# All steps of a recurrent attention and gated feed-forward kernel in another order

## The chip, the cores and the metric

The kernel runs on one core of a Trainium2 chip, from inputs in device memory to outputs in device memory, as one program. The metric is the device time of one execution in microseconds. Three runs of the kernel before took 202.21, 202.94 and 203.57 us; the median is 202.94.

## The reference

A linear attention with a per-channel decay (RWKV-6 form) is followed by a gated feed-forward layer. For 4 batches, 8 heads, 768 time steps and a head width of 48, the attention is

```python
for t in range(S):
    cur = np.einsum('bhd,bhe->bhde', u[None] * kt, vt)
    y[:, :, t] = np.einsum('bhd,bhde->bhe', rt, state + cur)
    state = wt[:, :, :, None] * state + np.einsum('bhd,bhe->bhde', kt, vt)
```

Its output, heads joined to rows of 384 (3072 rows), goes through

```python
rms = np.sqrt(np.mean(x * x, axis=-1, keepdims=True) + 1e-06)
xn = x / rms * rms_g
g = xn @ w_gate                       # 384 x 1536
silu = g * (1.0 / (1.0 + np.exp(-g)))
val = xn @ w_val                      # 384 x 1536
return (silu * val @ w_out)           # 1536 x 384
```

## The kernel before

**Tiles.** Time is cut into six superblocks of 128 steps (n = 0 to 5). A superblock holds the four batches (j = 0 to 3), so 4 x 128 = 512 rows go through the feed-forward layer together. The state of each batch is carried from one superblock to the next.

**Steps of the attention, per n and j.** `load_w`, `load_k`, `load_r`, `load_v` fetch 128 steps (lines 244 and 257; the first four `load_w` fetch superblocks 0 and 1 at once, all on SP's queue). `ln` takes the logarithm of w on ScalarE; `cs_mm` sums it along time on TensorE (for n of 2 and up `cs_add` on VectorE makes the second sum); `exp_r` and `exp_k` (ScalarE) turn the sums into factors, and `r_mul` and `k_mul` apply them (VectorE; `k_mul` on GpSimd for n of 1 and up). The products are transposed: for n = 0 and 1 by TensorE and a copy of ScalarE (`rk_pe`, `rk_tr`), later by a transposing DMA on SP's queue (`rk_tr`, line 474). `q_mm` multiplies them within the block, `q_mask_e`, `q_copy_o` and `q_mask_o` mask the result into SBUF; `cast_v` makes a bf16 copy of v (on ScalarE for n = 0 and 1, else on GpSimd); `y_mm` multiplies the masked result by it and adds the old state's part; `st_mm` and `st_new` make the new state. The term with u goes over `bonus_mul` (GpSimd, two products), `bonus_sum` (VectorE) and `bonus_v` (GpSimd), and `x_add` adds it to y.

**Norm.** `x_sq` (ScalarE), `x_rstd` (GpSimd, ScalarE for n = 0) and `xn_mul` (ScalarE) scale the rows; `xn_pe` with `xn_out` (n up to 3), or the transposing DMA `xn_tr` (line 563) with `xn_gain` on GpSimd (n = 4 and 5), put them transposed into `xnt`. A feed-forward step of superblock n needs the `xnt` of all four batches.

**Feed-forward, per n and f = 0 to 11** (columns of the weights in 12 parts of 128). `gate_mm` and `val_mm` are three matmuls of 128x512 each (line 598), called a group here; `silu` (ScalarE) and `h_mul` (VectorE) make `ht`. `o_mm` (line 630) multiplies all 12 parts of `ht` of one batch by `w_out` in 12 matmuls; `o_out` and `out_dma` copy and store it. The weights come by GpSimd's queue: `load_gv.g.h` (line 346) fetches a small piece (g = 0, f = 0 to 3) or a large one (g = 1, f = 4 to 11) of the gate (h = 0) or value (h = 1) weights, `load_wo` (line 352) the output weights.

**Zero matmuls.** `warm` (line 369) multiplies a tile of zeros and its result is not used. There are 48.

**What sets the order.** The string `ORDER` (lines 25 to 129) lists the 1106 steps one behind the other, and the loop of line 649 records them so. Nothing reorders them afterwards: each engine, SP's DMA queue included, takes its own steps in the order of the list and waits at each for what that step needs. Two other things follow from the list. The buffers of the pools are handed out in turn (eight for each of the loads of r, k and v, four for w). And `psum` (line 218) picks for each result of TensorE a bank that, by the list, has had its last use: two banks serve `cs_mm` and `gate_mm` (ring a), two `cs_mm`, `cs_add` and `val_mm` (b), four all else (q). So a `gate_mm` waits until the `silu` of the gate two before has emptied its bank.

`act` (line 227) puts an ACT_TABLE_LOAD ahead of a function of ScalarE that isn't in the table loaded last; `ln` and the exponentials are in one, `silu` in the other:

```python
def act(table_name, **kw):
    if table[0] != table_name:
        nc.scalar.preload_act_table_set(table_name)
        table[0] = table_name
```

## Time and profile before

| | |
|---|---|
| three runs, us | 202.21, 202.94, 203.57 |
| profiled execution: span from the first to the last instruction, us | 202.2 |
| TensorE busy, share of the span | 95% |
| VectorE, ScalarE, GpSimd busy | 72%, 68%, 66% |
| mean granted TensorE clock | 0.999 |
| read from device memory, written | 25.96 MB, 4.72 MB |
| function table loads of ScalarE | 10 |
| zero matmuls | 48 |

The profiled execution's span (202.2 us) is as long as the shortest run's time, so nothing that lies around the span has to be added to it. A row of a timeline or of the chain begins with the start and the duration in microseconds from the start of the span, then engine, line, operation, the tile written and the tiles read, and how many instructions stand in the row; in brackets is the idle time of the engine before it and what ended it. Matmuls are pipelined: their durations overlap, so their cost is read from one start to the next, or from the chain, which counts only the time that each adds. The rows of groups give the count, the busy time and the mean duration in nanoseconds, then the idle time in front and what ended most of it. "SPq" is SP's queue of DMA issues; a DMA issued by GpSimd is a row of GpSimd.

### The profile page before, as it was taken

The numbers are of one execution on the slowest core, as the hardware profiler recorded it, in microseconds if no ns is written. First come the engines' busy times: TensorE is split into PE (matmuls) and PEld (weight loads), VectorE is DVE, ScalarE is ACT, GpSimd is POOL, SyncE is SP. The second block draws the span as 40 slices with busy tenths as digits, with TensorE's granted clock in tenths as the row PEclk, the third lists the DMA queues.
The fourth block names the chain that finished last, engine by engine and source line by source line (L and its number), as shares of the span: only waits on it lengthen the run. The fifth ranks groups of instructions, "written<-read, shape, count | busy, mean of one in ns | idle before, by whom it ended". The sixth has DMA issues, their size and how long they took to land.

```text
span 202.2 us, 4444 instructions
## 1 busy us (share of the span) xinstructions
PE 192.6 (95%) x1600; PEld 113.5 (56%) x1600; DVE 146.1 (72%) x289; ACT 136.6 (68%) x278; POOL 134.3 (66%) x198
## 2 busy tenths in 40 slices
PE   1999988899999999999999999999999999999994
PEld 1564655455666555665556665555555555555562
DVE  6257796658999699987988889788878972146521
ACT  2577699688998557997566978679867764046300
POOL 6527599658789966899789898859898742400000
PEclk9999999999999999999999999999999999999999
DMA  6999999989999999958999978996184022103022
GB/s 152 243 244 177 209 182 202 202 161 201 199 192 221 196 179 238 225 133 194 177 231 245 206 171 195 216 241 134 24 192 112 15 68 71 45 3 117 0 97 99
DMA packets 121566, 32.41 MB, mean 160 GB/s; under 512 B 116420, under 2 KB 120392, under 8 KB 121544
## 3 DMA queue, kind: packets, MB, share of 16 engines
q1 hardware_dynamic: 119504, 28.58, 67.2%
q0 software_dynamic: 2032, 3.54, 9.7%
q8 instruction: 12, 0.20, 0.4%
q14 instruction: 10, 0.08, 0.1%
q10 hardware_dynamic: 8, 0.00, 0.0%
HBM read 25.96 MB, written 4.72 MB: 152 GB/s over the span
## 4 chain that ended last, share of the span: by engine, by line
PE 79%; SPq 8%; DMA 8%; POOL 2%; issue 1%; ACT 0%; POOLq 0%
PE ps_av L598 12%; PE ps_bu L598 12%; PE ps_bv L598 10%; PE ps_au L598 10%; PE ps_qx L630 8%; PE ps_qv L630 7%; SPq L244 7%; DMA wg_sb<-in_moe_w_gate_dram 6%; PE ps_qz L630 5%; PE ps_qu L630 3%; SPq L257 2%; DMA kt<-in_k_dram 2%; PE ps_qu L487 1%; PE ps_av L406 1%; PE ps_qu L515 1%
## 5 line engine op out<-in xcount | busy, mean ns | idle before, releaser
L630 PEld LDWEIGHTS <-ht 128*128 128x128 bf16 x300 | 28.3, 98 | 16.9
L231 ACT ACTIVATE sg<-ps_av 128x512 bf16<-128x512 f32 x38 | 22.7, 598 | 18.4 <-PE ps_av L598 16.8
L616 DVE TENSOR_TENSOR ht<-ps_bu,sg 128x512 bf16<-128x512 f32 x38 | 26.1, 686 | 11.7 <-PE ps_bu L598 8.4
L598 PEld LDWEIGHTS <-wg_sb 128*128 128x128 bf16 x216 | 22.8, 114 | 20.2 <-DMA wg_sb<-in_moe_w_gate_dram 2.1
L598 PEld LDWEIGHTS <-wv_sb 128*128 128x128 bf16 x216 | 23.2, 114 | 19.3 <-DVE xnt L580 0.2
L616 DVE TENSOR_TENSOR ht<-ps_bv,sg 128x512 bf16<-128x512 f32 x34 | 23.3, 686 | 12.2 <-PE ps_bv L598 8.8
L452 POOL TENSOR_TENSOR ruk<-rt,kt 128x384 f32<-128x384 f32 x24 | 24.0, 1000 | 11.1 <-DMA kt<-in_k_dram 6.0
L598 PE MATMUL ps_av<-xnt,wg_sb 128*128 128x512 bf16 x114 | 30.9, 380 | 0.4 <-DMA wg_sb<-in_moe_w_gate_dram 0.4
L231 ACT ACTIVATE sg<-ps_au 128x512 bf16<-128x512 f32 x34 | 20.4, 599 | 16.0 <-PE ps_au L598 14.6
L598 PE MATMUL ps_bu<-xnt,wv_sb 128*128 128x512 bf16 x114 | 30.9, 380 | 0.0
L598 PE MATMUL ps_au<-xnt,wg_sb 128*128 128x512 bf16 x102 | 27.7, 381 | 0.8 <-DMA wg_sb<-in_moe_w_gate_dram 0.8
L598 PE MATMUL ps_bv<-xnt,wv_sb 128*128 128x512 bf16 x102 | 27.7, 380 | 0.0
L453 POOL TENSOR_TENSOR ruk<-ruk,u_bc 128x384 f32<-128x384 f32 x24 | 23.9, 997 | 1.9
L462 POOL TENSOR_TENSOR ydiag<-vt,diag 128x384 f32<-128x384 f32 x24 | 19.7, 830 | 0.9 <-DVE diag L457 0.8
L446 POOL TENSOR_TENSOR rk<-kt,ek 128x384 bf16<-128x384 f32 x20 | 19.9, 1003 | 0.3 <-ACT ek L231 0.3
L505 POOL TENSOR_SCALAR_AFFINE_SELECT qts<-qts 128x512 bf16<-128x512 bf16 x20 | 12.5, 636 | 10.7 <-ACT qts L498 10.7
L630 PE MATMUL ps_qx<-wo_sb,ht 128*128 128x384 bf16 x96 | 16.9, 326 | 0.0
L630 PE MATMUL ps_qv<-wo_sb,ht 128*128 128x384 bf16 (+1 forms) x96 | 15.9, 316 | 0.0
L558 ACT ACTIVATE xn<-xb,rstd 128x384 bf16<-128x384 f32 x24 | 14.1, 608 | 1.2 <-POOL rstd L554 1.2
L457 DVE TENSOR_REDUCE diag<-ruk 128x8 f32<-128x384 f32 x24 | 12.9, 543 | 2.7 <-POOL ruk L453 2.7
L231 ACT ACTIVATE lw<-wt 128x384 bf16<-128x384 f32 (+1 forms) x20 | 11.2, 579 | 4.6 <-DMA wt<-in_w_dram 4.5
L229 ACT ACT_TABLE_LOAD x10 | 12.8, 1283 | 1.8 <-PEq L667 1.6
(153 smaller groups left out, 368.2 us busy)
## 6 DMA issues: line engine op xcount, KB each, us to landing
rt<-in_r_dram SPq DMA_DIRECT2D x24, 192.0 KB, 3.9
kt<-in_k_dram SPq DMA_DIRECT2D x24, 192.0 KB, 3.9
vt<-in_v_dram SPq DMA_DIRECT2D x24, 192.0 KB, 3.7
out_dram<-ob SPq DMA_DIRECT2D x23, 192.0 KB, 2.1
wt<-in_w_dram SPq DMA_DIRECT2D x16, 192.0 KB, 3.9
wt<-in_w_dram SPq DMA_DIRECT2D x4, 384.0 KB, 4.6
wo_sb<-in_moe_w_out_dram POOLq DMA_DIRECT2D x3, 384.0 KB, 5.2
wg_sb<-in_moe_w_gate_dram POOLq DMA_DIRECT2D x1, 768.0 KB, 12.0
```

Of the source, the lines that this page charges most:

```text
L229: nc.scalar.preload_act_table_set(table_name)
L231: return nc.scalar.activation(**kw).ins
L244: dmas["load_" + which, n, j] = nc.sync.dma_start(out=inp[which, n, j], in_=t[j, :, n * L:(n + 1) * L, :].rearrange("h t d -> t h d")).ins
L446: eng.tensor_tensor(out=rk[:, n % 2, j, 1, :, 0:D], in0=inp["k", n, j], in1=bank["cs_k", n, j][:, 0:DM].rearrange("p (h d) -> p h d", h=H) ...
L452: nc.gpsimd.tensor_tensor(out=ruk[n, j], in0=inp["r", n, j], in1=inp["k", n, j], op=ALU.mult)
L453: nc.gpsimd.tensor_tensor(out=ruk[n, j], in0=ruk[n, j], in1=u_bc, op=ALU.mult)
L457: nc.vector.tensor_reduce(out=diag[n, j].rearrange("p h o -> p (h o)"), in_=ruk[n, j], axis=mybir.AxisListType.X, op=ALU.add)
L462: nc.gpsimd.tensor_tensor(out=ydiag[n, j], in0=inp["v", n, j], in1=diag[n, j].to_broadcast([128, H, D]), op=ALU.mult)
L558: nc.scalar.activation(out=xn, in_=xb[n, j], func=AF.Copy, scale=rstd[n, j][:, 1:2])
L598: nc.tensor.matmul(ps, lhsT=units(ws, c, f), rhs=xnt[n][:, c, :], start=(c == 0), stop=(c == KC - 1))
L616: nc.vector.tensor_tensor(out=ht[n][:, f, :], in0=bank.pop(("v", n, f)), in1=bank.pop(("sg", n, f)), op=ALU.mult)
L630: nc.tensor.matmul(ps[:, cols], lhsT=ht[n][:, f, b * L:(b + 1) * L], rhs=wo_sb[:, f, cols], start=(f == 0), stop=(f == FC - 1))
```

## The change

The list is replaced by another of 1092 steps. All steps that compute, load or store are in both; the new one has 34 `warm` for 48. Everything else in the kernel is the same text, but the banks and buffers follow the new list.

- The 16 loads of superblock 0 come ahead of all loads of superblock 1 (before, two loads of superblock 1, `load_r.1.3` and `load_k.1.0`, stood ahead of the last, `load_k.0.3`). Batches of superblock 0 are taken in sequence 0, 1, 2, 3 (before 1, 0, 2, 3). The loads of v of superblock 1 are numbers 19, 26, 27 and 28 of SP's queue.
- GpSimd issues the weights as gate small, value small, gate large, value large (before: value small, gate small, gate large, value large); `bonus_v` of batches 2 and 3 of superblock 0 stands ahead of the first.
- The first feed-forward step is `gate_mm.0.1`, before it was `val_mm.0.2`. More attention steps of superblock 1 stand among the first groups.
- `ln.3.0`, `ln.3.1`, `ln.4.1` and `ln.5.1` stand among the `silu` of the superblock before: 16 table loads for 10.
- Of the four `o_mm.4`, two stand behind the first part of superblock 5's feed-forward steps.

The diff replaces all 105 lines of the list; here are the places spoken of:

```diff
-load_r.0.1 load_w.0.1 load_k.0.0 load_k.0.1 ln.0.1 warm.31.0 load_w.0.0 ln.0.0 warm.0.0 warm.13.0 warm.28.0
-bonus_mul.0.1 bonus_sum.0.1 load_r.0.0 load_v.0.0 bonus_mul.0.0 load_w.0.2 load_w.0.3 warm.29.0 load_k.0.2 load_v.0.1
-load_r.0.2 bonus_mul.0.2 load_r.0.3 load_v.0.3 load_v.0.2 bonus_v.0.1 load_r.1.3 load_k.1.0 cs_mm.0.1 exp_k.0.1
...
-rk_pe.0.1 warm.15.0 warm.14.0 load_k.0.3 bonus_mul.0.3 load_r.1.1 load_r.1.0 load_k.1.1 load_v.1.1 load_r.1.2 ln.0.3
-load_k.1.3 warm.20.0 warm.37.0 warm.2.0 warm.22.0 warm.23.0 warm.5.0 warm.3.0 rk_pe.0.0 warm.24.0 load_gv.0.1
-load_k.1.2 load_v.1.0 load_w.2.1 warm.25.0 load_v.1.2 load_w.2.0 load_v.1.3 load_r.2.1 load_r.2.0 load_w.2.2 warm.32.0
...
-exp_r.1.2 w_tot.1.2 r_mul.1.2 w_tot.1.3 bonus_mul.1.3 val_mm.0.2 val_mm.0.3 warm.46.0 gate_mm.0.2 gate_mm.0.3 rk_tr.1.1
-q_mm.1.1 silu.0.2 h_mul.0.2 load_k.2.0 silu.0.3 h_mul.0.3 bonus_sum.1.3 st_new.1.1 gate_mm.0.0 val_mm.0.1 rk_tr.1.0
-bonus_mul.1.0 val_mm.0.0 load_r.2.3 silu.0.0 q_mask_e.1.1 h_mul.0.0 bonus_mul.1.1 bonus_sum.1.1 gate_mm.0.6 silu.0.6
...
-gate_mm.4.10 silu.4.10 val_mm.4.10 h_mul.4.10 val_mm.4.11 h_mul.4.11 o_mm.4.1 o_mm.4.0 o_mm.4.2 x_rstd.5.2 xn_mul.5.2
-x_rstd.5.3 xn_mul.5.3 xn_tr.5.3 xn_tr.5.2 xn_gain.5.2 xn_gain.5.3 out_dma.3.3 xn_gain.5.1 o_mm.4.3 gate_mm.5.5 silu.5.5
...
+warm.0.0 warm.1.0 load_w.0.0 load_k.0.0 ln.0.0 load_w.0.1 cs_mm.0.0 warm.2.0 warm.3.0 warm.4.0 load_r.0.0 load_r.0.1
+exp_r.0.0 ln.0.1 cs_mm.0.1 load_w.0.2 r_mul.0.0 exp_k.0.0 w_tot.0.0 k_mul.0.0 load_k.0.1 rk_pe.0.0 warm.5.0 warm.6.0
...
+bonus_v.0.2 load_r.1.2 load_v.1.0 x_rstd.0.0 bonus_sum.0.3 cast_v.0.3 bonus_v.0.3 w_tot.1.1 st_new.0.0 q_mm.0.3
...
+xn_mul.0.1 load_k.1.0 load_r.1.1 y_mm.0.3 warm.32.0 x_sq.0.2 x_add.0.3 load_gv.0.0 x_sq.0.3 load_r.1.3 load_gv.0.1
+k_mul.1.1 xn_pe.0.1 cs_mm.1.2 x_rstd.0.2 r_mul.1.1 st_new.0.2 x_rstd.0.3 xn_mul.0.2 exp_r.1.2 xn_out.0.1 xn_pe.0.0
+xn_mul.0.3 k_mul.1.0 exp_k.1.2 st_mm.1.0 cs_mm.1.3 xn_pe.0.2 exp_r.1.3 xn_out.0.0 st_mm.0.3 warm.33.0 load_gv.1.0
+w_tot.1.2 xn_out.0.2 load_k.1.2 xn_pe.0.3 rk_pe.1.1 r_mul.1.2 xn_out.0.3 load_v.1.1 load_gv.1.1 load_v.1.3
...
+rk_pe.1.0 gate_mm.0.1 gate_mm.0.3 st_new.1.0 q_mm.1.1 silu.0.1 rk_pe.1.3 gate_mm.0.0 load_w.2.3 silu.0.3 val_mm.0.1
+load_r.2.0 bonus_mul.1.2 gate_mm.0.2 q_mask_e.1.1 rk_tr.1.3 val_mm.0.3 bonus_sum.1.0 rk_tr.1.0 q_copy_o.1.1 silu.0.2
+load_k.2.1 q_mm.1.0 h_mul.0.1 bonus_mul.1.1 val_mm.0.0 h_mul.0.3 q_mm.1.3 q_copy_o.1.0 load_w.2.2 rk_pe.1.2
+bonus_sum.1.1 val_mm.0.2 silu.0.0 q_mask_o.1.1 load_r.2.1 cast_v.1.1 q_mask_e.1.0 bonus_mul.1.3 y_mm.1.1 h_mul.0.0
+q_copy_o.1.3 load_r.2.2 gate_mm.0.5 rk_tr.1.2 h_mul.0.2 st_mm.1.1 bonus_v.1.1 gate_mm.0.6 q_mask_e.1.3 x_add.1.1
...
+gate_mm.1.5 val_mm.1.5 load_k.3.1 st_mm.2.0 silu.1.5 q_mask_o.2.0 val_mm.1.3 h_mul.1.5 gate_mm.1.11 st_new.2.0
+rk_tr.2.3 val_mm.1.8 bonus_v.2.3 h_mul.1.3 silu.1.8 ln.3.0 ln.3.1 gate_mm.1.4 y_mm.2.1 h_mul.1.8 silu.1.11 y_mm.2.0
+x_add.2.1 cast_v.2.2 val_mm.1.4 bonus_sum.2.2 st_mm.2.2 val_mm.1.11 bonus_v.2.0 load_r.3.0 silu.1.4 cast_v.2.3
+gate_mm.1.9 x_sq.2.1 x_add.2.0 st_new.2.2 out_dma.0.1 x_sq.2.0 load_r.3.1 x_rstd.2.1 load_k.3.3 load_r.3.2 silu.1.9
...
+val_mm.2.6 bonus_v.3.3 bonus_v.3.0 y_mm.3.0 val_mm.2.8 rk_tr.3.2 h_mul.2.6 load_k.4.3 val_mm.2.5 st_mm.3.2 ln.4.1
...
+gate_mm.4.7 y_mm.5.2 xn_tr.5.0 x_sq.5.3 x_rstd.5.1 silu.4.8 h_mul.4.0 val_mm.4.7 x_rstd.5.3 x_add.5.2 silu.4.7
+xn_mul.5.1 h_mul.4.7 x_sq.5.2 x_rstd.5.2 gate_mm.4.9 val_mm.4.8 xn_tr.5.1 gate_mm.4.10 val_mm.4.10 xn_mul.5.3
+xn_gain.5.0 h_mul.4.8 val_mm.4.9 silu.4.10 h_mul.4.10 xn_gain.5.1 xn_mul.5.2 xn_tr.5.3 silu.4.9 xn_tr.5.2 xn_gain.5.3
+h_mul.4.9 xn_gain.5.2 o_mm.4.1 o_mm.4.2 gate_mm.5.1 gate_mm.5.6 val_mm.5.6 silu.5.6 val_mm.5.1 gate_mm.5.2 silu.5.1
...
```

174 lines of the change are left out of this document (82 added, 92 removed).

## The prediction

> **What bounds the kernel now.** I read the page first, for the span, the busy shares and the chain that ended last.
>
> ```profile
> span 202.2 us, 4444 instructions
> ...
> PE 192.6 (95%) x1600; PEld 113.5 (56%) x1600; DVE 146.1 (72%) x289; ACT 136.6 (68%) x278; POOL 134.3 (66%) x198
> ...
> PE 79%; SPq 8%; DMA 8%; POOL 2%; issue 1%; ACT 0%; POOLq 0%
> ```
>
> TensorE is busy 95% of the span and makes up 79% of the chain; what is not TensorE there is loading and its issue. The chain in order of time says where each of them stands. From 39.90 to 199.3 us it holds nothing but matmuls, one behind the other. Two of its pieces give the pace:
>
> ```profile
> 163.58 0.65 PE ps_bu L598 x3
> ...
> 168.12 1.95 PE ps_qz L630 x12
> ```
>
> A group of three gate or value matmuls costs 0.65 us, twelve output matmuls of one batch cost 1.95 us. In that stretch there is no gap for an order to close; it can only open new ones. All that can be won lies ahead of it, and TensorE's timeline shows how little stands there:
>
> ```profile
> 33.19 0.81 PE L598 MATMUL ps_bu<-xnt,wv_sb 128*128 128x512 bf16 x3
> ...
> 34.48 0.33 PE L369 MATMUL ps_qz<-zero 128*128 128x384 bf16 x1
> 35.64 0.84 PE L598 MATMUL ps_au<-xnt,wg_sb 128*128 128x512 bf16 x3 [0.83 <-DMA wg_sb<-in_moe_w_gate_dram]
> ...
> 39.90 0.84 PE L598 MATMUL ps_av<-xnt,wg_sb 128*128 128x512 bf16 x3 [0.38 <-DMA wg_sb<-in_moe_w_gate_dram]
> ```
>
> The first value group runs at 33.19, the first gate group waits for its weights until 35.64, the first gate group of the second piece of weights until 39.90. Between 33.19 and 39.90 (6.71 us) the list holds seven groups (7 x 0.65) and one q_mm (0.33, next rows): 4.9 us. So 1.8 us are waiting. The smaller prices that I need, from the timeline:
>
> ```profile
> 37.06 0.23 PE L487 MATMUL ps_qz<-rkT 48*128 48x128 bf16 x1
> ...
> 37.39 0.84 PE L598 MATMUL ps_au<-xnt,wg_sb 128*128 128x512 bf16 x3
> ```
>
> and from the chain:
>
> ```profile
> 43.13 0.45 PE ps_qz L469 x8
> ...
> 156.85 0.17 PE ps_qv L532 x4
> 157.02 0.20 PE ps_qv L535 x8
> ```
>
> A q_mm of one batch takes 0.33 us (37.06 to 37.39), an rk_pe 0.45, a y_mm of a later superblock 0.17 + 0.20 = 0.37.
>
> **Zero matmuls.** Fourteen fewer. Two neighbours:
>
> ```profile
> 12.82 0.33 PE L369 MATMUL ps_qx<-zero 128*128 128x384 bf16 x1
> 12.98 0.33 PE L369 MATMUL ps_qz<-zero 128*128 128x384 bf16 x1
> ```
>
> They start 0.16 us apart, so 2.2 us of TensorE go. All stand ahead of 34.5 us, where TensorE waits for data anyway: I count nothing.
>
> **Loads and the weights' issue.** TensorE's work ahead of the first group is the same set in both orders: all of superblock 0, the running sums of superblock 1, two rk_pe and one st_mm of it. What can move is when that group starts. The weights are issued by GpSimd, in line with its products:
>
> ```profile
> 22.47 1.00 POOL L452 TENSOR_TENSOR ruk<-rt,kt 128x384 f32<-128x384 f32 x1 [3.39 <-DMA kt<-in_k_dram]
> ...
> 24.49 0.99 POOL L346 DMA_DIRECT2D wv_sb<-in_moe_w_val_dram  x1
> ...
> 26.29 0.81 POOL L346 DMA_DIRECT2D wg_sb<-in_moe_w_gate_dram  x1
> ...
> 27.90 0.80 POOL L346 DMA_DIRECT2D wg_sb<-in_moe_w_gate_dram  x1
> ```
>
> Before, the issue waits for bonus_mul.0.3, and that 3.39 us for load_k.0.3, the 18th load on SP's queue. In the new order superblock 0 is complete with the 16th load, so the product can start some 2 us earlier. But the gate weights now stand behind bonus_v.0.2 and bonus_v.0.3 as well, and these wait for bonus_sum on VectorE, where masks, products and a state update are put ahead. The trace does not show that mixture; the issue cannot come earlier than 22.5 - 2 + 2 products + 2 x 0.8 = 24 us, and I bound it at 26.3, where the gate weights are issued today. I take 24.5, the nearest row.
>
> ```profile
> wg_sb<-in_moe_w_gate_dram POOLq DMA_DIRECT2D x1, 768.0 KB, 12.0
> wv_sb<-in_moe_w_val_dram POOLq DMA_DIRECT2D x1, 768.0 KB, 13.5
> wv_sb<-in_moe_w_val_dram POOLq DMA_DIRECT2D x1, 384.0 KB, 7.5
> wg_sb<-in_moe_w_gate_dram POOLq DMA_DIRECT2D x1, 384.0 KB, 9.3
> ```
>
> The first small piece lands 7.5 us after its issue: first gate group at 24.5 + 7.5 = 32.0, about 1 us before today's first group. The second small piece follows GpSimd's next slot, and the first large piece comes behind two k_mul, about where it is today (27.90 + 12.0 = 39.9).
>
> Up to gate_mm.0.5, the first that needs a large piece, the new order has eight groups, three q_mm, two rk_pe and one y_mm: 8 x 0.65 + 3 x 0.33 + 2 x 0.45 + 0.37 = 7.5 us. From 32.0 that is 39.5, so it arrives just as the large piece lands. Where today's TensorE stands at 39.9 with 4.9 us of this work done, the new one would stand there with 7.5: **2.6 us won**, if nothing else is late.
>
> **What is late next.** That y_mm.1.1 needs load_v.1.1, which ScalarE converts first. It is the 26th load of SP's queue. Today the 26th is load_v.1.0:
>
> ```profile
> L244 SPq DMA_DIRECT2D vt<-in_v_dram x1: 1305/1305/1305, 25.6 to 25.6; - x1
> ...
> DMA to landing us min/median/max: 15.1/15.1/15.1
> ```
>
> A cast of v is this group of ScalarE:
>
> ```profile
> L374 ACT CAST vb<-vt x8: 490/504/515, 13.0 to 51.6; 128x384 bf16<-128x384 f32 x8
> ```
>
> It lands 15.1 us after its issue at 25.6, at 40.7, since the weights hold the DMA engines. The DMA view of 34 to 40 us shows how:
>
> ```profile
> q0 software_dynamic: 565, 1.10, 97.3%
> q1 hardware_dynamic: 562, 0.11, 16.5%
> ```
>
> The weights' queue and SP's move equally many packets (565, 562), but 1.10 MB against 0.11 MB. Today nothing urgent stands at that place, for y_mm.1.0 comes eight groups behind the one at 39.90. In the new order ScalarE waits there, with the copies and silus queued behind cast_v.1.1 on it, and TensorE at y_mm.1.1: 40.7 + 0.5 for the cast puts it at 41.3 and gate_mm.0.5 at 41.7. By 41.7 today's kernel has done 4.9 + 1.8 = 6.7 us of that work, the new one 7.5. I keep **0.8 us won**; one end is 2.6 (the load slips in ahead of the weights). The other is the load behind it today, load_w.2.1, issued at 27.1:
>
> ```profile
> DMA to landing us min/median/max: 17.6/17.6/17.6
> ```
>
> It lands at 44.7; with v.1.1 as late, gate_mm.0.5 would come at 45.7, when today's kernel has done 10.7 us of work, and 3.2 us would be lost.
>
> The Trainium skill, "DMA: Bandwidth & Descriptors", section "Queues, rings and completion order", says that each DMA engine takes turns between queues by whole packets. The two packet counts above agree. By that rule the move of v behind other loads of superblock 1 is bad whatever the weights' place, and the sum would keep the 0.8; without it, by an even split of bytes, it would be 2.6.
>
> **ScalarE's table loads.** The new order puts ln.3.0/3.1, ln.4.1 and ln.5.1 between silus, and each needs the other function table and back: 16 loads for 10.
>
> ```profile
> L229 ACT ACT_TABLE_LOAD x10 | 12.8, 1283 | 1.8 <-PEq L667 1.6
> ```
>
> The next rows are from TensorE's and ScalarE's timelines, and from the table of stretches (busy us of TensorE, its weight loads, VectorE, ScalarE, GpSimd):
>
> ```profile
> 175.75 0.81 PE L598 MATMUL ps_au<-xnt,wg_sb 128*128 128x512 bf16 x3
> ```
>
> ```profile
> 113.44 0.94 ACT L231 ACTIVATE lw<-wt 128x384 bf16<-128x384 f32 x2
> ...
> 176.60 0.60 ACT L231 ACTIVATE sg<-ps_au 128x512 bf16<-128x512 f32 x1 [7.50 <-PE ps_au L598]
> ```
>
> ```profile
> 80.00:100.00 20.00, 20.00 (x185) 12.27 (x182) 17.72 (x39) 16.20 (x34) 17.45 (x24) 1.00 0.97 191
> ```
>
> Six more are 7.7 us of ScalarE, which is busy 16.20 of 20 us in this stretch. A silu starts 0.2 us behind its group (175.75 + 0.65 to 176.60) and takes 0.60. At the first pair, counted from the end of gate_mm.1.5: 0.2, silu.1.5 and silu.1.8 1.2, load 1.28, two ln 0.94, load 1.28, silu.1.11 0.6 make 5.5 us. TensorE meanwhile has seven groups, two y_mm and two st_mm (four matmuls, 0.17 each): 5.6 us before gate_mm.1.9 needs that bank. It is covered with 0.1 us to spare; by the same count the other two pairs, with one ln each, have 0.3 and 0.7. Cost: nothing when ScalarE is in step, up to the whole block of about 3.2 us (two loads and the ln) for each pair when it isn't. I take 0.4 for all three together, nearer to the covered end, as ScalarE today mostly waits for TensorE.
>
> **The last superblock.** Today four o_mm.4 stand between the last attention step and gate_mm.5; the new order leaves two there and moves two behind. From the last y_mm to gate_mm.5.1 TensorE has six groups and two o_mm: 3.9 + 3.9 = 7.8 us. What it must cover, x_add to the scaled xnt, took for two batches (timelines of VectorE, GpSimd and SP, and the DMA issues with the median to landing):
>
> ```profile
> 157.26 0.56 DVE L540 TENSOR_TENSOR xb<-ps_qv,ydiag 128x384 f32<-128x384 f32 x1
> ...
> 161.92 0.55 DVE L540 TENSOR_TENSOR xb<-ps_qx,ydiag 128x384 f32<-128x384 f32 x1
> ```
>
> ```profile
> 164.53 0.83 POOL L586 TENSOR_TENSOR xnt<-xnt,gT 128x384 bf16<-128x384 bf16 x1 [0.30 <-DMA xnt<-xn]
> ```
>
> ```profile
> 164.90 1.19 SPq L563 DMA_TRANSPOSE xnt<-xn  x1
> ```
>
> ```profile
> xnt<-xn SPq DMA_TRANSPOSE x8, 2.7
> ```
>
> Batch 5.0: 157.26 to 165.36, 8.1 us. Batch 5.1: 3.0 to its transpose, 2.7 to landing, 0.83 to scale, 6.5 us. Against 7.8 this costs 0 to 0.3, plus what other batches on SP's queue add; I take 0.2. The end behind the last o_mm is the same in both orders.
>
> **The sum.** 202.2 - 0.8 + 0.4 + 0.2 = 202.0 us against the profiled execution, whose span equals the lowest of the three runs (202.21); the median shown is 0.7 higher, so **202.7 us** in its terms. A measurement of this kernel tells about 1% (2.0 us) from no change.
>
> **The rivals.**
> - *The whole ramp is won.* load_v.1.1 lands ahead of the weights, or the cast waits little: 202.9 - 2.6 + 0.2 = 200.5. For it: the issue at GpSimd may be a little later than SP's 26th. Against it: 15.1 us at that very place. Chance 0.22.
> - *The table pairs are not covered* (slower). Once ScalarE is over 0.1 us behind at the first pair, gate_mm waits for its bank, and half of three blocks of 3.2 us, 4.8, lands on TensorE: 202.9 - 0.8 + 4.8 = 206.9; the point where it passes 1% is 2.8 us of such waits. For it: 0.1 and 0.3 are thin, and GpSimd, which makes the masks that y_mm needs in the same stretches, is busy 17.45 of 20. Against it: 7.50 us in front of the silu quoted above are a wait for TensorE, not the other way round. Chance 0.28.
> - *The order doesn't do what it says.* Gate weights are first among the weights, but later in GpSimd's line; issued at 26.3, they give the first group at 33.8 and, if the large piece shifts by as much, gate_mm.0.5 at 41.4, when today's kernel has done 6.4 us against 7.5: 202.9 - 1.1 + 0.6 = 202.4. So this alone decides little. Chance 0.10, within 1%.
>
> **How the numbers follow.** Forecast 0.40 and the last rival 0.10 lie within 1%: same 0.50. Faster 0.22, slower 0.28. The range runs from the whole ramp won with little added (200.3) over the late load (202.9 + 3.2 + 0.2 = 206.3) to just short of the uncovered pairs.
>
> **What would show it.** In the new profile: the first matmul of L598 near 32 us; the first with ps from the large piece near 41.7 rather than 39.9, ScalarE idle in front of a cast of vt from about 39 until 41; 16 table loads; TensorE's pieces from 42 us on without gaps, or with gaps in front of L598 released by silu at the reload pairs; a gap ahead of the first L598 of superblock 5 under 0.5 us. A load of v.1.1 that lands by 33, or gaps of over 3 us in total behind 45, prove me wrong.

## The result, and the profile after

| | before | after |
|---|---|---|
| median of the runs, us | 202.63 (202.16 to 203.57, 5 runs) | 212.95 (209.66 to 216.27, 5 runs) |
| ratio, 95% interval | | 1.036 (1.032 to 1.041) |
| profiled execution, span, us | 202.2 | 211.2 |

The changed kernel is slower by 3.6%, outside the predicted range of 200.3 to 206.3 us. The ratio after rests on the two executions at 209.66 and 210.44, whose mean granted clock was 0.99 or more, while the profile is of the one at 212.95 us (clock 0.983). One correction comes first. The five executions after list a span beside each time (211.2 for 212.95, 208.0 for 209.66): the time is 1.7 us longer than the span. The prediction took span and time to be equal, which was wrong; by the same difference the profiled execution of before, with a span of 202.2, took about 203.9 us.

The page of the changed kernel, its first lines, the row of TensorE's granted clock in 40 slices, the shares of the chain, and three groups:

```profile
span 211.2 us, 4416 instructions
...
PE 192.8 (91%) x1586; PEld 113.1 (54%) x1586; DVE 146.3 (69%) x289; ACT 143.8 (68%) x284; POOL 134.7 (64%) x198
...
PEclk9999999967999999999999999999999999999999
...
PE 63%; DMA 12%; SPq 11%; DVE 4%; POOL 4%; issue 2%; ACT 2%; DVEq 0%; ACTq 0%; POOLq 0%
...
L446 POOL TENSOR_TENSOR rk<-kt,ek 128x384 bf16<-128x384 f32 x20 | 19.9, 1001 | 9.3 <-DMA kt<-in_k_dram 6.8
...
L229 ACT ACT_TABLE_LOAD x16 | 20.5, 1283 | 1.9 <-PEq L667 1.6
...
L457 DVE TENSOR_REDUCE diag<-ruk 128x8 f32<-128x384 f32 x24 | 13.0, 543 | 7.0 <-POOL ruk L453 7.0
```

TensorE was 79% of the chain and is 63%; loads and their issue have risen from 16 to 23%. The clock row has a dent in two slices, at 42 to 53 us. And two groups name what was waited for: GpSimd's products of k (L446) stood idle 6.8 us for a load of k, VectorE's row sums (L457) 7.0 us for GpSimd.

The ramp in the timelines of TensorE, GpSimd, VectorE and ScalarE (start, duration, ..., idle time before and what ended it):

```profile
32.71 0.62 PE L598 MATMUL ps_au<-xnt,wg_sb 128*128 128x512 bf16 x2 [0.31 <-DMA wg_sb<-in_moe_w_gate_dram]
...
40.85 0.40 PE L469 MATMUL ps_qz<-ident,rk 128*128 128x128 bf16 x4 [1.43 <-POOL rk L446]
...
46.09 0.48 PE L532 MATMUL ps_qv<-st,rkT 128*128 128x96 bf16 x4 [4.19 <-DVE qts L494]
```

```profile
24.60 0.99 POOL L346 DMA_DIRECT2D wg_sb<-in_moe_w_gate_dram  x1
25.60 0.79 POOL L346 DMA_DIRECT2D wv_sb<-in_moe_w_val_dram  x1
```

```profile
44.88 0.55 DVE L457 TENSOR_REDUCE diag<-ruk 128x8 f32<-128x384 f32 x1 [6.42 <-POOL ruk L453]
45.35 0.68 DVE L494 TENSOR_TENSOR qts<-ps_qv,mask_lt 128x512 bf16<-128x512 f32 x1
```

```profile
44.20 0.51 ACT L374 CAST vb<-vt 128x384 bf16<-128x384 f32 x1 [5.05 <-DMA vt<-in_v_dram]
```

The first group comes at 32.71 us, as predicted. Then TensorE waits 1.43 us in front of rk_pe.1.2 and 4.19 us in front of y_mm.1.1 (46.09). The chain says why:

```profile
24.67 15.06 DMA kt<-in_k_dram
...
39.80 0.99 POOL rk L446
40.80 0.97 POOL ruk L452
...
43.85 1.01 POOL ruk L453
...
45.35 0.69 DVE qts L494
...
46.09 0.48 PE ps_qv L532 x4
46.57 0.32 PE ps_qv L535 x8
46.88 1.28 PE ps_av L598 x3
48.17 0.32 PE ps_qx L515 x4
48.49 1.28 PE ps_au L598 x3
...
50.31 0.84 PE ps_av L598 x3
```

load_k.1.2, the 25th load on SP's queue, is issued at 24.67, a few hundredths of a microsecond behind the first piece of the weights (24.60), and lands 15.06 us later. GpSimd works in order: k_mul.1.2 stands ahead of bonus_mul.1.2 and 1.1, so these start only at 40.80. VectorE works in order too: bonus_sum.1.1 waits for the second of them, and behind it stands q_mask_e.1.0, whose bank y_mm.1.1 needs. load_v.1.1 is late as well (the cast starts at 44.20), but the mask is later. Behind the gap a group takes 1.28 us in place of 0.65. The stretches of the same kernel show the clock (columns as in the prediction: busy us of TensorE, its weight loads, VectorE, ScalarE, GpSimd; clock; DMA share; GB/s):

```profile
43.00:44.00 1.00, 0.00 (x0) 0.00 (x0) 0.00 (x0) 0.00 (x0) 0.92 (x2) 0.81 0.24 48
44.00:46.00 2.00, 0.00 (x0) 0.00 (x0) 1.11 (x3) 1.80 (x3) 2.00 (x3) 0.50 0.61 123
46.00:48.00 2.00, 1.91 (x16) 1.07 (x16) 1.83 (x4) 0.11 (x1) 1.92 (x3) 0.50 1.02 202
48.00:50.00 2.00, 2.00 (x16) 0.88 (x14) 1.59 (x3) 0.80 (x2) 1.98 (x4) 0.50 0.92 182
50.00:52.00 2.00, 2.00 (x24) 1.10 (x21) 0.00 (x0) 1.21 (x3) 1.94 (x4) 0.89 0.93 131
```

While TensorE idles the granted clock goes to 0.50, and it stays there until about 50.4 us. From 46.09 to 50.31 stand a y_mm, two groups, an st_mm and a q_mm, by the prices in the prediction 0.37 + 1.30 + 0.16 + 0.33 = 2.2 us of work: 2.1 us more.

Behind the ramp, what TensorE waited for from 60 to 180 us (us in all, times, longest):

```profile
PE ps_qz L630 <- DVE ob L637: 1.7, 1, 1.7
PE ps_au L598 <- POOL xnt L586: 0.6, 1, 0.6
PE ps_au L406 <- ACT lw L231: 0.2, 1, 0.2
```

So this execution has 1.4 + 4.2 us of idle time and 2.1 us of half clock in the ramp, and 1.7 + 0.6 + 0.2 behind it: 10.2 us. The waits of before that they replace were 0.8 + 0.4. That makes 9.0, the difference of the two spans (211.2 - 202.2). That it fits to a tenth is partly luck: short waits in both ramps, and the earlier start of the groups, are left out.

This accounts for the profiled execution. No trace exists of those at 209.66 and 210.44; what can be said of them stands under "The changed kernel once more".

### The profile page after: what moved, and what is told of

Read it like the earlier page. It is cut to its first block, busy times and chain, and to the rows that moved or that the text cites. A ratio compares the mean times of both kernels' runs of the same rounds, so it can differ in the third digit from the quotient of the medians.

```text
span 211.2 us, 4416 instructions
## 1 busy us (share of the span) xinstructions
PE 192.8 (91%) x1586; PEld 113.1 (54%) x1586; DVE 146.3 (69%) x289; ACT 143.8 (68%) x284; POOL 134.7 (64%) x198
## 4 chain that ended last, share of the span: by engine, by line
PE 63%; DMA 12%; SPq 11%; DVE 4%; POOL 4%; issue 2%; ACT 2%; DVEq 0%; ACTq 0%; POOLq 0%
PE ps_au L598 10%; PE ps_av L598 10%; SPq L244 9%; PE ps_bu L598 9%; PE ps_bv L598 8%; DMA kt<-in_k_dram 7%; PE ps_qx L630 5%; PE ps_qz L630 4%; PE ps_qu L630 4%; PE ps_qv L630 4%; DMA vt<-in_v_dram 3%; SPq L257 2%; DVE ht L616 2%; DMA out_dram<-ob 2%; POOL rk L446 1%
## 5 line engine op out<-in xcount | busy, mean ns | idle before, releaser
L616 DVE TENSOR_TENSOR ht<-ps_bu,sg 128x512 bf16<-128x512 f32 x37 | 25.4, 686 | 10.9 <-PE ps_bu L598 8.2
L616 DVE TENSOR_TENSOR ht<-ps_bv,sg 128x512 bf16<-128x512 f32 x35 | 24.0, 686 | 11.5 <-PE ps_bv L598 9.5
L231 ACT ACTIVATE sg<-ps_av 128x512 bf16<-128x512 f32 x36 | 21.6, 599 | 14.9 <-PE ps_av L598 14.2
L598 PE MATMUL ps_au<-xnt,wg_sb 128*128 128x512 bf16 x108 | 30.0, 387 | 0.9 <-POOL xnt L586 0.6
L598 PE MATMUL ps_bu<-xnt,wv_sb 128*128 128x512 bf16 x111 | 30.1, 380 | 0.0
L598 PE MATMUL ps_av<-xnt,wg_sb 128*128 128x512 bf16 x108 | 30.0, 388 | 0.0
L231 ACT ACTIVATE sg<-ps_au 128x512 bf16<-128x512 f32 x36 | 21.5, 598 | 10.4 <-PE ps_au L598 8.5
L446 POOL TENSOR_TENSOR rk<-kt,ek 128x384 bf16<-128x384 f32 x20 | 19.9, 1001 | 9.3 <-DMA kt<-in_k_dram 6.8
L229 ACT ACT_TABLE_LOAD x16 | 20.5, 1283 | 1.9 <-PEq L667 1.6
L457 DVE TENSOR_REDUCE diag<-ruk 128x8 f32<-128x384 f32 x24 | 13.0, 543 | 7.0 <-POOL ruk L453 7.0
L630 PE MATMUL ps_qu<-wo_sb,ht 128*128 128x384 bf16 x84 | 14.8, 326 | 0.0
L545 ACT ACTIVATE junk<-xb 128x384 bf16<-128x384 f32 x24 | 12.5, 519 | 2.4 <-DVE xb L540 2.1
L630 PE MATMUL ps_qx<-wo_sb,ht 128*128 128x384 bf16 (+1 forms) x84 | 13.8, 314 | 0.0
```

The source lines that it names most:

```text
L231: return nc.scalar.activation(**kw).ins
L446: eng.tensor_tensor(out=rk[:, n % 2, j, 1, :, 0:D], in0=inp["k", n, j], in1=bank["cs_k", n, j][:, 0:DM].rearrange("p (h d) -> p h d", h=H) ...
L457: nc.vector.tensor_reduce(out=diag[n, j].rearrange("p h o -> p (h o)"), in_=ruk[n, j], axis=mybir.AxisListType.X, op=ALU.add)
L598: nc.tensor.matmul(ps, lhsT=units(ws, c, f), rhs=xnt[n][:, c, :], start=(c == 0), stop=(c == KC - 1))
L616: nc.vector.tensor_tensor(out=ht[n][:, f, :], in0=bank.pop(("v", n, f)), in1=bank.pop(("sg", n, f)), op=ALU.mult)
L630: nc.tensor.matmul(ps[:, cols], lhsT=ht[n][:, f, b * L:(b + 1) * L], rhs=wo_sb[:, f, cols], start=(f == 0), stop=(f == FC - 1))
```

## The experiments

Times are medians with lowest and highest; each is compared with the kernel before on the same chip (its medians were 202.95 to 203.68 us). Edits are shown as steps of the list; "..." stands for steps between that stay.

**Which load, which line.** Three edits of the ramp.

e_v11:
```diff
-load_v.1.0 ... cast_v.1.0 ... st_mm.1.0 ... st_new.1.0 ... load_v.1.1 ... cast_v.1.1 ... gate_mm.0.4 ... y_mm.1.0
+load_v.1.1 ... cast_v.1.1 ... load_v.1.0 ... cast_v.1.0 gate_mm.0.4 ... st_mm.1.0 st_new.1.0 y_mm.1.0
```

> The changed order with load_v.1.1 and load_v.1.0 exchanged on SP's queue (v.1.1 becomes the 19th load, v.1.0 the 26th); cast_v.1.1 takes the place of cast_v.1.0, and cast_v.1.0, st_mm.1.0 and st_new.1.0 go down to y_mm.1.0. Theory A (the late 25th load, load_k.1.2, holds GpSimd, and through it the mask that y_mm.1.1 needs): y_mm.1.1 still starts near 46.1 us and the gap ahead of it stays near 4.2 us; the time stays within 1 us of the changed order (209.7 to 213). Theory B (the wait is that of the prediction, load_v.1.1 alone): y_mm.1.1 starts near 42 us, the gap is under 0.5 us, and the time falls by 4 us or more, to 206 or less.

Measured: 214.68 us (206.69 to 216.75). In its trace y_mm.1.1 starts at 47.35, after 4.18 us of idle time, although v.1.1 had been there for long. GpSimd's row:

```profile
41.08 0.99 POOL L446 TENSOR_TENSOR rk<-kt,ek 128x384 bf16<-128x384 f32 x1 [8.05 <-DMA kt<-in_k_dram]
```

The early load of v did not close the gap in this execution: theory A holds for it and the prediction's theory B falls, though the time is above the 209.7 to 213 that theory A gave. One execution of the four ran at 206.69, and no trace shows what it looked like.

e_k12:
```diff
-k_mul.1.2 ... bonus_mul.1.2 ... rk_pe.1.2 ... bonus_mul.1.3 y_mm.1.1 ... gate_mm.0.5 rk_tr.1.2
+bonus_mul.1.3 k_mul.1.2 bonus_mul.1.2 y_mm.1.1 ... gate_mm.0.5 rk_pe.1.2 rk_tr.1.2
```

> The changed order with k_mul.1.2 and bonus_mul.1.2 moved behind bonus_mul.1.3 on GpSimd, and rk_pe.1.2 behind gate_mm.0.5 on TensorE; the loads stay. Theory A and B together (both loads are late, either one holds y_mm.1.1): GpSimd runs on through bonus_mul.1.1 from about 32 us, no mask waits for it any more, and y_mm.1.1 waits for the cast of load_v.1.1, 44.2 + 0.6 = 44.8 us instead of 46.1: 1.3 us faster at equal clock (208.4). Theory A alone: the gap goes, y_mm.1.1 near 42, 4 us faster (205.7). Theory B alone: nothing changes.

Measured: 211.28 us (210.17 to 213.42), ratio 1.037 (1.032 to 1.042). GpSimd is free now, y_mm.1.1's first half (with the state) runs near 40, and its second half waits for the cast of v.1.1:

```profile
44.06 0.36 PE L535 MATMUL ps_qz<-vb,qts 128*128 128x48 bf16 x8 [3.75 <-ACT vb L374]
```

As A and B together had it in the trace: either load alone is enough for a gap of about 4 us. The time of 208.4 was not reached.

e_both, with both edits:

> The changed order with both edits of the two runs before. Loads A and B together: y_mm.1.1 near 42 us, no gap over 0.5 us there, no half clock behind it; 209.7 - 4.2 = 205.5 us, and at most 203.5 if the half clock cost another 2 us in every run. If the ramp's loss is something else (weights landing, banks), the time stays above 208.

Measured: 211.60 us (209.16 to 213.14), ratio 1.032 (1.026 to 1.037). A miss, and an instructive one. GpSimd issued the first piece at 24.31 here, and now the 24th load, r.1.3 (issued 24.55), was behind it:

```profile
37.21 0.56 DVE L440 TENSOR_TENSOR rk<-rt,ps_av 128x384 bf16<-128x384 f32 x1 [5.67 <-DMA rt<-in_r_dram]
```

It is not a matter of this load or that, but of where the loads that are needed soon stand in time against the start of the weights.

**The clock.** One step of 26 zero matmuls into one bank of the ring of gate groups:

```diff
+warm_a.26.0
 y_mm.1.1
```

> The changed order with one step of 26 zero matmuls (26 x 0.16 = 4.2 us) in front of y_mm.1.1, in a bank that is free there. They save no wait: y_mm.1.1 still starts near 46.1 us. Theory: the idle stretch halves TensorE's clock behind it in some executions (0.5 from 43.4 to 50.2 us in the profiled one, some 2 us and more). Then the clock stays 1.00 here, every run lies near 209 to 210, and the slow ones of 212 to 216 are gone. Rival (the clock falls for another reason, and varies by itself): the runs scatter from 209 to 216 as before.

Measured: 208.76 us (207.31 to 212.79), ratio 1.024 (1.019 to 1.029). In the profiled execution the clock stays at 1.00 through the ramp though GpSimd waits for load_k.1.2 until 38.4, so zero matmuls in a wait can hold it. Three executions lie at 207.3 to 209.3, one at 212.79 with a mean clock of 0.992, so they may not hold it always; that execution has no trace.

**The order of issue.** If it decides, moving GpSimd's issue behind SP's must free the loads, and moving it ahead must starve those of the kernel before.

e_gvlate:
```diff
-load_gv.0.0 ... load_gv.0.1 k_mul.1.1 ... k_mul.1.0 ... load_gv.1.0
+k_mul.1.1 ... k_mul.1.0 load_gv.0.0 load_gv.0.1 ... load_gv.1.0
```

> The changed order with load_gv.0.0 and load_gv.0.1 (the two small pieces of the weights) moved behind k_mul.1.0 on GpSimd: all four pieces are then issued from about 26.5 us on, when SP has issued its 25th and 26th load. Theory (a load of SP's queue issued after the first piece of the weights is starved, one issued before is not): load_k.1.2 and load_v.1.1 land near 29 to 31 us in place of 39.7 and 44.2, the first gate group comes 2 us later (34.7), y_mm.1.1 starts near 41.8 in place of 46.1 without a gap of over 1 us, no half clock follows, and every run lies near 205.4 us (209.7 - 4.3), the clock at 1.00. Rival (the queue's own length holds them: they land 15 us after issue whatever the weights do): the gap of 4.2 us stays, and the 2 us come on top: 211.7 or more.

Measured: 209.01 us (207.66 to 209.42), ratio 1.028 (1.024 to 1.033). load_v.1.1, issued at 26.11, lands at 30.1; nothing waits at y_mm.1.1, and the scatter of 7 us is gone. But the first gate group waits 1.90 us for its weights (34.61), the clock is at half from about 34 to 37.5 us, and behind the ramp TensorE waits 2.33 us for an output buffer (for 1.70 in the changed kernel). That the late loads make the gap at y_mm.1.1 is confirmed. The gain of 4 us is not there: the ratio lies between the two that the changed kernel gave (1.036, and 1.023 in the last runs below); what is gone are its executions of 212 us and more.

e_gv1, by one product only:
```diff
-load_gv.0.0 ... load_gv.0.1 k_mul.1.1
+k_mul.1.1 load_gv.0.0 load_gv.0.1
```

> The changed order with load_gv.0.0 and load_gv.0.1 moved behind k_mul.1.1 only, by one product: the first piece of the weights is issued near 25.6 us, load_k.1.2 (25th on SP) near 24.7 and load_v.1.1 (26th) near 25.7. Theory (what counts is whether a load is issued before the first piece, and a few tenths of a us decide it): load_k.1.2 lands by 33 us, load_v.1.1 near 39 to 40; y_mm.1.1 then starts near 41 and TensorE has no gap of over 1 us there, as the prediction had it for load_v.1.1 alone. The clock stays at 1.00 in most runs, and most runs lie near 206 to 207.5. Rival (load_k.1.2 is starved by the weights whether it is issued before or behind them): it lands near 39, the gap of 4 us stays, the runs scatter from 209 to 216 as those of the changed order.

Measured: 210.21 us (209.09 to 211.78), ratio 1.035 (1.031 to 1.039). In its trace the weights are issued at 27.04 (k_mul.1.1 itself waited 1.08 us for its load), load_k.1.2 at 26.05; TensorE has no gap at y_mm.1.1. The ramp is repaired, and yet the kernel is no faster than the better executions of the changed one. What TensorE waited for from 60 to 180 us in it:

```profile
PE ps_qz L630 <- DVE ob L637: 2.2, 1, 2.2
PE ps_qv L630 <- DVE ob L637: 1.4, 1, 1.4
PE ps_au L598 <- POOL xnt L586: 1.3, 1, 1.3
PE ps_au L598 <- ACT sg L231: 0.3, 1, 0.3
```

5.2 us in place of 2.5: some 2.7 us of what the ramp wins is lost again behind it.

b_k03, on the kernel before:
```diff
-load_r.1.3 load_k.1.0 ... load_k.0.3
+load_k.0.3 load_r.1.3 load_k.1.0
```

> The kernel before with load_k.0.3 as the 16th load in place of the 18th (load_r.1.3 and load_k.1.0 one place down each): bonus_mul.0.3 and with it the first piece of the weights can be issued 1.5 to 2 us earlier, near 22.7 us. Theory of the starved loads: then the 23rd to 26th load of SP's queue (r.1.2, k.1.3, k.1.2, v.1.0) are issued behind the weights and land 10 to 15 us later; r_mul.1.2 or k_mul.1.3 waits for them, and the time is level or 1 to 4 us longer, with more scatter. Rival (earlier weights are worth their time): 1 to 2 us faster than before, 201.5 to 202.5.

Measured: 209.55 us (203.20 to 211.53), beside 202.98 for before. The first piece is issued at 22.51 instead of 24.49. In GpSimd's and SP's timelines:

```profile
22.51 0.99 POOL L347 DMA_DIRECT2D wv_sb<-in_moe_w_val_dram  x1
...
41.15 0.98 POOL L453 TENSOR_TENSOR ruk<-rt,kt 128x384 f32<-128x384 f32 x1 [10.79 <-DMA kt<-in_k_dram]
```

```profile
24.47 4.74 SPq L245 DMA_DIRECT2D kt<-in_k_dram  x2
```

load_k.1.3, issued at 24.47, holds GpSimd for 10.79 us until 41.15; TensorE waits 4.75 us, and its clock falls to half. One load moved up by two places brings the kernel before to 209 to 211.5 us in three executions of four; the fourth ran at 203.20, level with before, and has no trace. In the kernel before, load_k.1.3 was issued 0.62 us ahead of the first piece and landed 4.0 us later; here it is issued 1.96 us behind it.

How late a load comes is not settled by which of the two issues is first. In the kernel before, load_k.1.2 was issued 0.35 us behind the first piece (24.49) as well:

```profile
24.84 0.76 SPq L244 DMA_DIRECT2D kt<-in_k_dram  x1
```

It had landed by 32.5, after 7.7 us; with the changed kernel's GpSimd, free for it at 32.95, that would have cost nothing. The traces of all runs together give a slope and not a step. Loads of 192 KB issued at least 1 us ahead of the first piece landed 3.4 to 5.0 us after their issue, those within 1 us ahead of it 3.6 to 9.0, those within 1 us behind it 6.2 to 17.8, and those 1 to 4 us behind it 12.2 to 18.5. Of the loads within 1 us behind, those of the kernel before and its variants (s_rest and s_rest_tab below among them), where the second piece follows 1.80 us behind the first, took 6.2 to 10.6 us; those of the changed kernel and its variants, where it follows 1.00 us behind, took 9.6 to 17.8. So the two small pieces that the new list issues back to back are a second suspect beside the place of the load. No run changed that distance alone, so it is not shown.

**Ramp and rest apart.** The list of one kernel up to its first o_mm.0.0, then all steps that are left in the order of the other.

> The changed order up to its first o_mm.0.0, then all steps that are left in the order of before. If the loss is made in the ramp alone, the time is that of the changed order, 209.7 and above. By the trace, 2.5 to 3 us of it are made behind the ramp (1.7 in front of an output batch near 126 us, 0.6 near 157, 0.4 before 120): then 206.7 to 207.2 at equal clock, with the same scatter upward by the half clock.

Measured: 209.19 us (204.45 to 211.51). The profile is of the execution at 204.45. Its ramp is that of the changed kernel, step for step, but GpSimd came a little later:

```profile
24.67 0.73 SPq L244 DMA_DIRECT2D kt<-in_k_dram  x1
```

```profile
25.38 0.99 POOL L346 DMA_DIRECT2D wg_sb<-in_moe_w_gate_dram  x1
...
32.74 1.96 POOL L446 TENSOR_TENSOR rk<-kt,ek 128x384 bf16<-128x384 f32 x2
```

```profile
39.60 0.51 ACT L374 CAST vb<-vt 128x384 bf16<-128x384 f32 x1
```

load_k.1.2 is issued at 24.67 as in the changed kernel, but the weights at 25.38 in place of 24.60. The two k_mul run through at 32.74, v.1.1 is cast at 39.60, y_mm.1.1 runs at 40.70 and gate_mm.0.5 at 41.08, with no gap and at full clock:

```profile
40.70 0.33 PE L532 MATMUL ps_qv<-st,rkT 128*128 128x96 bf16 x4
...
41.08 0.82 PE L598 MATMUL ps_av<-xnt,wg_sb 128*128 128x512 bf16 x3
```

So the ramp of the new order has at least two outcomes, and 0.8 us of GpSimd's time lies between these two.

> The reverse: the order of before up to its first o_mm.0.0, then all steps that are left in the changed order (15 table loads). By the trace 2.5 to 3 us are lost behind the ramp: 202.8 + 2.7 = 205.5, every run at a clock of 1.00 and within 1 us of the others, since the gap that halves the clock is not there. If the ramp made the whole loss: 202.8. If the table loads cost by themselves what the prediction's slower rival said (4.8): 207 and above.

Measured: 207.86 us (207.23 to 208.65), ratio 1.024 (1.020 to 1.028). With the ramp of before the scatter is small, and 4.6 us are lost against the 203.25 of before, more than the 2.7 expected. TensorE's waits from 40 to 180 us:

```profile
PE ps_qv L631 <- DVE ob L638: 1.7, 1, 1.7
PE ps_qv L570 <- ACT xn L559: 1.7, 1, 1.7
```

The second, at 56 us, lies at the joint of the two lists and belongs to neither; the first is the output buffer again. The time is one that the expectation gave to the rival of the table loads, but TensorE waits for a silu 0.2 us in all here, so the table loads don't make it. Some 2.9 us are left for the rest of the changed order, by the trace of the changed kernel 2.5.

s_rest_tab:
```diff
-ln.3.0 ln.3.1 ... cs_mm.3.1 silu.1.10 ... cs_mm.3.0
+silu.1.10 ln.3.0 ln.3.1 ... cs_mm.3.1 cs_mm.3.0
...
-ln.4.1 ... silu.2.10
+silu.2.10 ln.4.1
...
-ln.5.1 ... cs_mm.5.1 ... silu.3.10 ... cs_mm.5.0
+silu.3.10 ln.5.1 ... cs_mm.5.1 cs_mm.5.0
```

> The run before, with ln.3.0, ln.3.1, ln.4.1 and ln.5.1 behind the last silu of their stretch, and cs_mm.3.1 and cs_mm.5.1 moved along: 9 table loads for 15. Theory (the table loads are covered; the loss behind the ramp is the late output transfers and the last superblock): the time stays within 0.5 us of the run before. Rival (the table loads hold TensorE's banks): 2 to 5 us faster than the run before.

Measured: 211.53 us (209.38 to 213.92), ratio 1.033 (1.027 to 1.038): slower, not faster, than with the 15 loads (209.38 and 209.94 at a clock of 1.00, against 207.86). TensorE waits 2.6 us in three places for these very logarithms (ps_av L407 <- ACT lw L232). Six table loads between the silus are covered; logarithms that come late are not. The prediction's slower rival, table loads that hold TensorE's banks, is out.

**Output buffers.** o_out writes to one of three buffers, and a buffer is free when its out_dma has run. In the changed list the out_dma of superblocks 1 and 2 stand up to 179 steps behind their o_out (1.0: 179, 1.3: 130, 1.2: 106; before 54, 3 and 138).

```diff
-out_dma.1.2 ... out_dma.1.3 ... out_dma.1.0
+out_dma.1.1 out_dma.1.0 ... w_tot.3.2 out_dma.1.2 ... h_mul.2.1 out_dma.1.3
```

e_out has this edit on e_gvlate:

> The changed order with the weights' issue behind k_mul.1.0 as in the run above, and out_dma.1.0, 1.2 and 1.3 each moved up SP's list to a few steps behind its o_out. Theory (the gap of 1.7 to 2.5 us in front of an output batch of superblock 2 is o_out.2.0, which waits for one of three output buffers, held by transfers that stand late on SP's queue): that gap goes, 2.3 us faster than the run above (209.0): 206.7. Rival (the gap is TensorE's, from late xnt or a bank of another step): the gap stays and the time too.

Measured: 207.52 us (206.17 to 208.70), ratio 1.019 (1.013 to 1.025), against 1.028. The wait of 2.3 us in front of the output batch at 121 us is gone from the trace; one of 1.3 us at the start of superblock 4's groups is left. The ratio fell by 0.9% (1.9 us), though the two intervals still touch.

e_out1 has it on the changed kernel, alone:

> The changed order with out_dma.1.0, 1.2 and 1.3 early as the only edit, the weights' issue where the change has it. Theory: the gap of 1.7 to 2.3 us in front of o_mm.2.3 goes; by the scatter of the ramp the runs still reach from 208 to 214, the lower end 1.5 to 2 us below that of the changed kernel (209.7 to 207.9). Rival: it comes back in another place, no change.

Measured: 211.95 us (210.16 to 213.83), ratio 1.034 (1.029 to 1.040): no gain, a miss. The wait for ob is gone here too, but the ramp's is not. In this trace load_k.1.2 is issued 0.22 us behind the first piece (25.57 and 25.35) and lands at 35.2, load_v.1.1 at 44.12; TensorE's waits from 40 to 180 us:

```profile
PE ps_qv L535 <- ACT vb L374: 2.8, 1, 2.8
PE ps_au L598 <- POOL xnt L586: 1.3, 1, 1.3
PE ps_qv L532 <- DVE qts L494: 0.7, 1, 0.7
```

**Zero matmuls, and all repairs.** Fourteen zero matmuls in one step, on e_gvlate:

```diff
+warm_a.14.0
 gate_mm.0.1
```

> The changed order with the weights' issue behind k_mul.1.0, and the fourteen zero matmuls back, in one step in front of gate_mm.0.1. Theory (TensorE idles from about 31 to 34.6 us, and the clock falls to half behind it: four groups at 1.28 us for 0.65): with 2.3 us of that filled, the clock stays at 1.00, 1.3 to 2 us faster than without (209.0): near 207.3, and so the fourteen zero matmuls are not free of effect as the prediction took them. Rival (the clock does not hang on idle time, or zero matmuls do not count): no change.

Measured: 209.68 us (207.30 to 210.03, 5 runs), ratio 1.030 (1.027 to 1.034), as without them (1.028). The profiled execution (207.30) kept a clock of 1.00, the other four show 0.992. Inconclusive: the zero matmuls can hold the clock here, and did so once in five.

e_fix has all three edits (weights behind k_mul.1.0, outputs early, fourteen zero matmuls):

> The changed order with all three edits: weights' issue behind k_mul.1.0, fourteen zero matmuls back, output transfers early. If the causes add up: 209.0 - 2.3 - 1.7 = 205.0, within 1 us; the rest to the kernel before (2 us) is the first group 2 us later and the gap of 1.3 us at the start of superblock 4's groups. If they overlap, 206 to 207.

Measured: 205.96 us (205.03 to 206.87), ratio 1.012 (1.007 to 1.016), clock 1.00 in all four executions. The three edits win back two thirds of the changed kernel's 3.6%, or half of the 2.3% of its last runs below. e_fix1 is the same with the weights' issue of e_gv1:

> The run before, with the fourteen zero matmuls back in front of gate_mm.0.1 and out_dma.1.0, 1.2 and 1.3 early. If the causes found so far are all, and the 2.4 us that three edits left were mostly the first group coming 2 us late (weights issued at 27.3), this is 1 us faster than those three edits: 205.0, clock 1.00. If what is left lies in the later superblocks, it is again 206.

Measured: 206.69 us (205.18 to 207.09), ratio 1.016 (1.012 to 1.021). This doesn't test an earlier first group: the weights are issued 0.64 us earlier than in e_fix, but the fourteen zero matmuls stand in front of the first group, and it starts at 35.59 in this trace, at 35.01 in that of e_fix. In e_fix TensorE waits 1.3 us in three places between 40 and 180 us; the remaining microsecond isn't pinned down, and the first group, 1.8 us behind that of the kernel before (33.19), may be part of it.

**Gate weights first, alone.** On the kernel before:

```diff
-load_gv.0.1 ... load_gv.0.0 ... val_mm.0.2 val_mm.0.3 warm.46.0 gate_mm.0.2 gate_mm.0.3
+load_gv.0.0 ... load_gv.0.1 ... gate_mm.0.2 gate_mm.0.3 val_mm.0.2 val_mm.0.3 warm.46.0
```

> The kernel before with one part of the change alone: the gate weights' small piece issued ahead of the value weights', and gate_mm.0.2 and 0.3 ahead of val_mm.0.2 and 0.3. Theory: the second piece is waited for as before, only with the names exchanged (0.83 us ahead of the third group); within 0.5 us of before. Rival (gate first costs or wins by itself): over 1 us of difference.

Measured: 204.02 us (202.95 to 204.62, 10 runs), ratio 1.001 (0.998 to 1.004): no difference.

**The changed kernel once more.**

> The changed kernel itself once more, for a trace of an execution near 210 us. Theory (two outcomes of one race): if load_k.1.2 is issued ahead of the first piece of the weights, the ramp has no gap at y_mm.1.1, the clock stays at 1.00, and what is lost lies behind: 1.5 near 91, 2.3 near 122 and 1.3 us near 154, as in the kernel with the weights one product later (209.7). If it is issued behind, the gap of 4 us is there and the gaps behind are smaller (2.7 in all). Rival: the gap of 4 us is there in the executions near 210 us as well, and only the half clock differs.

> The changed kernel once more, a second look, with the same two outcomes of the race and the same rival as the run before.

Measured: 208.27 us (207.53 to 219.37, 4 runs), ratio 1.023 (1.018 to 1.028), and one execution at 216.31. The profiles are of the executions at 219.37 and 216.31. In the first the weights (24.90) are ahead of r.1.3 (25.32) as well as of k.1.2 (26.29), and TensorE waits 1.35 us for r.1.1 (issued at 24.18, landed at 29.8), 1.23 us for r.1.3 and 4.19 us behind k.1.2; in the second (24.73 against 25.42 for k.1.2) GpSimd's row is

```profile
42.32 0.99 POOL L446 TENSOR_TENSOR rk<-kt,ek 128x384 bf16<-128x384 f32 x1 [9.24 <-DMA kt<-in_k_dram]
```

and TensorE waits 4.03 and 3.84 us. What an execution of the changed kernel near 208 to 210 us looks like was not caught and stays open. By the traces with its ramp or nearly so (s_ramp 204.45, e_out1 210.40, e_gv1 209.66) it can be one with a shorter gap, or one with none and more waiting behind. That the ratio of 1.023 is that of s_rest (1.024), which has the ramp of before, speaks for the second; it isn't shown. An estimate says the same: before's 202.95, less the 0.8 that the forecast gave to a ramp without this gap, with the 5.2 us that e_gv1 waits behind its ramp, make 207.4, beside the 207.53 and 207.86 measured at a clock of 1.00. If that is so, these executions lose their time to output buffers and late transposes and not to the loads of the ramp.

## Why the prediction was wrong

**Dense TensorE, only the ramp to win, gaps to lose.** The picture was right: the loss is gaps, and the half clock behind one of them. The price wasn't. New gaps behind the ramp were put at 0.6 us (0.4 for the table loads, 0.2 for the last superblock) and everything else there at nothing; the traces show 2.5 us in the changed kernel and 5.2 in e_gv1, hardly any of it at those two places. The equality of span and time was wrong by 1.7 us.

**Zero matmuls at nothing.** Not refuted for the place where they stood: the profiled executions keep the clock at 1.00 up to the first group, at 32.71, with 34 of them. Their price was taken as TensorE's time alone; that they also hold the clock was left out; e_warm's profiled execution shows that they can.

**Weights' issue.** Right. Taken at 24.5, it came at 24.60; first gate group 32.0, it came at 32.71; the large piece 39.9, it landed at 39.4. What the prediction didn't see is that the issue time, which it let run from 24 to 26.3, is not a small uncertainty but decides over the whole ramp: at 24.60 it comes ahead of SP's 25th load (24.67, landed at 39.7), at 25.38 (s_ramp) 0.7 us behind it, and nothing waits for that load.

**"What is late next".** This is the step that failed, in two places. First, it looked at one load and its own reader. It took load_v.1.1, the 26th, for the only one that is late and never asked for the 25th, although that is load_k.1.2 in both lists. Before, k_mul.1.2 stood behind a mask on GpSimd and ran at 43.17, when its load had long landed (32.5); in the new list it stands ahead of bonus_mul.1.2, bonus_mul.1.1 and q_mask_o.1.1. The step named what is queued behind cast_v.1.1 on ScalarE, and left out what is queued behind k_mul.1.2 on GpSimd and, behind bonus_sum.1.1, on VectorE. The wait that ends last is this one (4.19 us, ended by the mask), not the cast. Second, v.1.1 was mis-sized: taken at 40.7 from today's 26th, it landed at 44.2 (43.5 and 44.1 in e_k12 and e_out1). Today's 26th is issued at 25.64 ahead of the second piece of the weights (26.29), the new one at 25.65 just behind it (25.60). Luck is in the size of it too: in s_ramp the same load landed at 38.8, in time. The bound of 44.7 held for the load, but its price of 3.2 us did not: the idle time in the ramp is 5.6 us in the profiled execution, and the half clock adds 2.1.

The rule of round robin by packets (the Trainium skill, "DMA: Bandwidth & Descriptors", "Queues, rings and completion order"), which the prediction weighed, agrees with its two packet counts (565 and 562). It holds for whatever SP's queue carries, so it could have pointed to the 25th load too. It doesn't say how late a load comes: the 25th landed 7.7 us after its issue before and 15.06 after the change, though it was issued behind the first piece in both.

**Table loads.** Right: 16, each 1283 ns, no gap of TensorE at the three pairs; a cost of 0.4 was taken, none was seen. The rival that priced them at 4.8 us ended on the right side (206.9 for 209.7 and more) for a wrong reason.

**The last superblock.** Superblock 5 starts without a gap. The same chain, transposes on SP's queue, is late at superblock 4 (0.6 us in the changed kernel, 1.3 in e_gv1 and e_out1), which the prediction didn't work out.

**What no step had.** The output transfers: the prediction followed the loads on SP's queue, but not the out_dma that stand on the same queue. The three buffers cost 1.7 us in the changed kernel and up to 3.6 where the ramp is repaired.

**The rivals.** The forecast's own ramp, without even its wait for v.1.1, exists as an outcome: in s_ramp's profiled execution y_mm.1.1 runs at 40.70 and gate_mm.0.5 at 41.08, where the forecast had 41.3 and 41.7. It is the other outcome of a race that the prediction saw only for the 26th load (under "The whole ramp is won"). "The order doesn't do what it says" was not the case.

## What to carry to other kernels

Where a large transfer starts on a second DMA queue, list every load that the first queue issues within a microsecond of it, not the one that looks urgent; for each, follow its consumer and all that is queued behind that consumer on its engine, and on the engines that wait for those. If a few tenths of a microsecond decide on which side of the start a needed load falls, count on both outcomes and give it a place with some slack; here a microsecond ahead of the start was enough. Stores that free buffers belong on that list as well.
